# Where the sums of x live and when they are queued: mirrored-exponentials buffers for blocks 3 to 6, a later place for batch 0, and weight sums in sixteen short additions

## The chip, the cores and the metric

The kernel runs on one core of one Trainium2 chip. The metric is device microseconds (us) of one execution; lower is better. A core has a matrix engine (TensorE, PE in the profile, with its weight loads as PEld), a vector engine (VectorE, DVE), an activation engine (ScalarE, ACT), a general engine (GpSimd, POOL) and a queue engine that issues DMAs (SyncE, SP). Each engine works through its own list of instructions in order: an instruction that waits holds up everything queued behind it on that engine.

## The reference, cut to what matters

```python
# attention, per batch of 8: z [3008, 64], u and v [3008, 256]
scores = (1.0 / S) * np.matmul(z, z.transpose(0, 2, 1))
attn = np.maximum(scores, 0.0) ** 2
x = u * np.matmul(attn, v)                         # [8, 3008, 256]
# mixer on x: over tokens, then over channels
h = np.maximum(x.transpose(0, 2, 1) @ w_tok1, 0.0) @ w_tok2     # w_tok1 [3008, 256]
u2 = x + h.transpose(0, 2, 1)
out = u2 + np.maximum(u2 @ w_ch1, 0.0) @ w_ch2                  # w_ch1 [256, 1536]
```

## The kernel before, in words

The work of a batch is cut into six blocks of 512 tokens (the last has 448); block numbers q run from 0 to 5 in the code, so "blocks 3 to 6" of the title are q = 2 to 5. For each block the scores against six groups of keys are made on PE (`sc`, L439), passed through ReLU on ACT into tiles `at` (L477, L465) and squared on DVE in place (L485, L517). The score matrix is symmetric, so from batch 1 on (in batch 0 all are computed) a tile above the diagonal is also transposed by a DMA into a tile `fl` (L537, function `flip`) and used a second time for the mirrored block; these are the "mirrored exponentials" of the change's short title. PE multiplies the tiles with v (`acc`, L668). DVE adds the two halves of the result (`cp`, L805) and multiplies by the transposed u (`xT`, L825). A DMA transpose on SP turns each block of xT into x (L854, function `turn_x`).

The mixer of a batch then runs in pieces on PE. The token product `tok1` (L965) multiplies x by w_tok1, seven products of 128x128 tiles in the place of eight, for each pair of token tiles; it is six pieces, one for each block, of 14 matmuls each. The seven products need sums of the four sub-blocks of x and of the weights. The sums of x are four short subtractions on DVE for each block, each needing the one before (L885, function `x_sums`), into a tile `d`. The sums of the weights are made once (L917 to L920, function `token_sums`) from w_tok1 into `w_sum_sb`. When the six pieces of tok1 are done, `collect_a` (L977) gathers the result on DVE into `a_sb` (seven instructions, L988 to L994); then come the six pieces of `tok2` (L1012), then ReLU layers `hp` (L1066) and the channel products, `xb` and `zb` (L1194) by sums of their own (`hsum`, L1145 to L1157) and `op` (L1280); the results are added up in tiles `ro` (L1231).

From batch 1 on, x is turned only when the v buffers of the batch come free, at the end of its last block, and all six blocks are turned one behind the other. In that stage PE works off the rest of the mixer of the batch before (its blocks 3 to 5: hp, xb, zb), then tok1, collect_a and tok2 of its own batch with what is left of that rest in between.

The order on all engines is fixed when the program is built, by a planner in the kernel. PE's clock is kept in `pe[0]`; work for ACT, DVE and SP is put into lists by `push(engine, ready, busy, lat, fn, first, room, done, frees)`, and `next_op` takes the operation that can start first (the largest `first` wins a tie, so operations with `first=-1` fill what is left). `room` names buffer pools that must have a free place, or a test. An operation of the mixer is a `Piece` with the events that it `needs`; PE takes the next piece whose events are due, and goes on in the same list (`heads` for tok1 and tok2, `tails` for the rest) while one is `opened`: tok1 opens with its first piece and closes with its last. A planned time is a guess: `turn_x` counts 7.5 us from issue to landing (12.0 for the last block). The instruction itself waits for the real event.

The pools that matter here, as `ROOM` has them: `xd`, two buffers for sums of x; `h2`, five; `fl`, ten, for mirrored tiles, for hsum, for ro, for the scratch of collect_a and, in batch 0, for v. In batch 0 the sums of q = 0 to 3 lie two by two in `h2` tiles (`d_pair`); all others take an `xd` buffer each, so that from batch 1 on the sums of q = 2 need tok1 of q = 0 to be over, and so on:

```python
        push("dve", t, 0.21, 0.36, lambda t: x_sums(b, q, t), first=-1,
             room=() if in_h2(b, q) else ("xd",))
...
            live["xd"] -= not in_h2(b, q)          # at the end of tok1 of block q
```

Of the kernel before, what the change touches and what calls it, by code (L numbers as in the profile page):

```python
# [9 lines left out]
BF16 = mybir.dt.bfloat16  # L10
# [3 lines left out]
P = 128  # L14
# [43 lines left out]
def kernel(  # L58
# [11 lines left out]
    nc = tc.nc  # L70
# [4 lines left out]
    KT = (S + P - 1) // P  # L75
# [5 lines left out]
    NQ = (S + QW - 1) // QW  # L81
# [6 lines left out]
    sb = ctx.enter_context(tc.tile_pool(name="sb", bufs=2))  # L88
    psum = ctx.enter_context(tc.tile_pool(name="psum", bufs=2, space=bass.MemoryType.PSUM))
    first = ctx.enter_context(ExitStack())  # L90
# [12 lines left out]
    w_sum_sb = consts.tile([P, 3, KT // 2, P], BF16)  # L103
# [221 lines left out]
    live = {"at": 0, "fl": 0, "xT": 0, "xd": 0, "h2": 0, "us": 0}  # L325
    ROOM = {"at": 6, "fl": 10, "xT": 9, "xd": 2, "h2": 5, "us": 2}
    v_free = [NG]
    at_free = [0.0] * ROOM["at"]
    fl_free = [0.0] * ROOM["fl"]
    ring = [(Done(0.0), i) for i in range(RING)]  # L330
# [7 lines left out]
    def push(engine, ready, busy, lat, fn, first=0, room=(), done=None, frees=()):  # L338
        op = Op(ready, busy, lat, fn, first, room, done, frees)
        waiting[engine].append(op)  # L340
        return op.done
# [34 lines left out]
    pe = [0.0]  # L376
# [165 lines left out]
    def release(name, uses, t=0.0):  # L542
        uses[0] -= 1
        uses[1:] = [max([t] + uses[1:])]
        if not uses[0]:
            live[name] -= 1
            if name == "at":
                at_free.append(uses[1])
            if name == "fl":
                fl_free.append(uses[1])  # L550
# [283 lines left out]
            push("sp", t, 1.25, 7.5 if q < NQ - 1 else 12.0, lambda t: turn_x(b, q, t), first=1,  # L834
                 room=lambda: b == 0 or (mode[0] == "full" and v_free[0] > 0))

    x_pair, d_pair = [], []

    def in_h2(b, q):

        return b == 0 and q < NQ - 2

    def turn_x(b, q, t):

        if b == 0:
            if q % 2 == 0:
                x_pair[:] = [sb.tile([P, 2, DT, QW // P, P], BF16, tag="h2", name="x_pair",
                                     bufs=ROOM["h2"])]
                live["h2"] += 1
            x = x_pair[0][:, q % 2]  # L850
        else:
            x = sb.tile([P, DT, QW // P, P], BF16, tag="v", name="x_sb", bufs=NG)
            v_free[0] -= 1
        nc.sync.dma_start_transpose(  # L854
            out=x.rearrange("p h t d -> p (h t) d"),
            in_=xTs[b, q].rearrange("p h s -> p (h s)"))
        xs[b, q] = x
        x_done[b, q].t = t
        push("dve", t, 0.21, 0.36, lambda t: x_sums(b, q, t), first=-1,
             room=() if in_h2(b, q) else ("xd",))  # L860

    xds = {}
    xd_done = {(b, q): Done() for b in range(B) for q in range(NQ)}

    def x_sums(b, q, t):


        shape = [P, 3, QW // P // 2, P]
        if in_h2(b, q):
            if q % 2 == 0:  # L870
                d_pair[:] = [sb.tile([P, 2] + shape[1:], BF16, tag="h2", name="d_pair",
                                     bufs=ROOM["h2"])]
                live["h2"] += 1
            d = d_pair[0][:, q % 2]
        else:
            live["xd"] += 1
            d = sb.tile(shape, BF16, tag="xd", name="xd", bufs=ROOM["xd"])
        xds[b, q] = d
        v = xs[b, q].rearrange("p n (j r) d -> p n j r d", r=2)
        low, high = v[:, :, :, 0, :], v[:, :, :, 1, :]  # L880
        steps = [(d[:, 1], high[:, 1], low[:, 1]), (low[:, 1], low[:, 1], low[:, 0]),
                 (d[:, 0], high[:, 1], low[:, 1]), (d[:, 2], high[:, 0], d[:, 0])]

        def step(t):
            nc.vector.tensor_sub(*steps.pop(0))  # L885
            if steps:
                push("dve", t - 0.1, 0.21, 0.36, step, first=-1,
                     done=None if len(steps) > 1 else xd_done[b, q])

        step(t)  # L890
# [18 lines left out]
    mix_done, tok_mix_done = Done(), Done()  # L909
    eaten = {b: 0 for b in range(B)}  # L910

    def token_sums(t):


        w = w_tok1_sb.rearrange("p (j r) (m t) -> p j r m t", r=2, t=P)
        low, high = w[:, :, 0], w[:, :, 1]
        nc.vector.tensor_sub(w_sum_sb[:, 0], low[:, :, 0, :], low[:, :, 1, :])  # L917
        nc.vector.tensor_sub(w_sum_sb[:, 1], high[:, :, 1, :], w_sum_sb[:, 0])
        nc.vector.tensor_sub(w_sum_sb[:, 2], high[:, :, 0, :], w_sum_sb[:, 1])
        nc.vector.tensor_add(low[:, :, 1, :], low[:, :, 1, :], high[:, :, 1, :])  # L920
    late_sums = []

    def mix_weights(t):
# [9 lines left out]
    def add_mixer(b):  # L933
# [8 lines left out]
        def tok1(q, end):  # L942

            if q == 0:
                st["a_slot"], _ = take_slot()
                st["a_ps"] = bank_pair(st["a_slot"], "a_ps").rearrange(
                    "p r (k d) -> p r k d", d=P)
            a_ps = st["a_ps"]
            x, d = xs.pop((b, q)), xds.pop((b, q))
            w = w_tok1_sb.rearrange("p (j r) (m t) -> p j r m t", r=2, t=P)  # L950
            n = QW // P // 2
            xp = x.rearrange("p n (j r) d -> p n j r d", r=2)
            for i in range(n):
                j = q * n + i
                products = [
                    ((0, 0), w[:, j, 0, 0, :], xp[:, 0, i, 0, :]),
                    ((0, 1), w[:, j, 1, 0, :], xp[:, 0, i, 1, :]),
                    ((1, 1), w[:, j, 0, 1, :], xp[:, 1, i, 0, :]),
                    ((0, 2), w_sum_sb[:, 1, j, :], d[:, 0, i, :]),
                    ((1, 2), w_sum_sb[:, 0, j, :], d[:, 1, i, :]),  # L960
                    ((0, 3), w_sum_sb[:, 2, j, :], xp[:, 1, i, 1, :]),
                    ((1, 0), w[:, j, 1, 1, :], d[:, 2, i, :]),
                ]
                for (r, k), lhs, rhs in products:
                    nc.tensor.matmul(  # L965
                        a_ps[:, r, k, :], lhs, rhs, start=(j == 0 and (r, k) in ((0, 0), (1, 1))),
                        stop=(j == KT // 2 - 1), skip_group_check=True)
            live["xd"] -= not in_h2(b, q)
            if b == 0:
                live["h2"] -= q % 2 * (1 + in_h2(b, q))  # L970
            else:
                v_free[0] += 1
            eaten[b] = q + 1
            if q == NQ - 1:
                home = "fl" if b else "h2"

                def collect_a(t):  # L977
                    live[home] += 1
                    if b:
                        fl_free.pop(0)  # L980
                    f = sb.tile([P, 8, P], F32, tag=home, name="a_f", bufs=ROOM[home])

                    def both(to, ps, k):
                        nc.vector.tensor_add(  # L984
                            f[:, to:to + 2, :], ps,
                            f[:, k:k + 1, :].to_broadcast([P, 2, P]))

                    nc.vector.tensor_copy(f[:, 6, :], a_ps[:, 0, 0, :])  # L988
                    both(0, a_ps[:, 0, 1:3, :], 6)
                    both(4, a_ps[:, 1, 1:3, :], 1)  # L990
                    nc.vector.tensor_add(f[:, 1, :], a_ps[:, 0, 3, :], f[:, 4, :])
                    both(2, a_ps[:, 1, 0:2, :], 5)
                    st["a"] = sb.tile([P, 2, D], BF16, tag="a", name="a_sb", bufs=1)
                    nc.vector.tensor_single_scalar(  # L994
                        st["a"].rearrange("p m d -> p (m d)"),
                        f[:, 0:4, :].rearrange("p k d -> p (k d)"), 0.0, AX.max)
                    recent[0] = st["a"][:, 0, :1]
                    a_done.t = t
                    if b:
                        release("fl", [1], t)  # L1000
                    else:
                        live["h2"] -= 1
                ring.append((push("dve", end + 0.21, 1.7, 1.9, collect_a, first=1,
                                  room=(home,), frees=fl_free if b else ()), st["a_slot"]))

        def tok2(q, end):
# [318 lines left out]
        for q in range(NQ):  # L1325
            heads.append(Piece(0.784, [x_done[b, NQ - 1], xd_done[b, q], tok_mix_done],
                               lambda end, q=q: tok1(q, end),
                               opens=q < NQ - 1, closes=q > 0, key=(b, 0)))
        for q in range(NQ):
            heads.append(Piece(4 * column_time(widths[q]), [a_done, tok2_done[q]],  # L1330
                               lambda end, q=q: tok2(q, end), key=(b, 1)))
# [269 lines left out]
    def ask_w_tok1(c):  # L1601
        load_w_tok1(c)
        if c == NG - 1:
            push("dve", pe[0] + 16.0, 3.9, 4.1, token_sums, done=tok_mix_done)

    def ask_w_tok2(c):
        load_w_tok2(c)
# [42 lines left out]
    while cur[0] is not None or heads or tails:  # L1650
        run_engines(pe[0])
        ask_some()
        t = pe[0]
# [15 lines left out]
        n = can_score(done_units, most)  # L1669
# [12 lines left out]
        low = lead <= 3  # L1682
# [42 lines left out]
        if pick is None:  # L1725
# [4 lines left out]
            op = next_op()  # L1730
# [15 lines left out]
        elif pick == "av":  # L1746
            step = (blk.b * NQ + blk.q) * NG + blk.slot
# [40 lines left out]
```

## Time and profile before

| | before |
|---|---|
| Median of 3 runs | 1145.62 us (1144.76 to 1146.49) |
| The profiled execution | 1146.74 us |
| Its span, first to last instruction | 1144.9 us |
| PE busy | 1124.2 us (98%) |
| DVE busy | 792.3 us (69%), 1832 instructions |
| ACT busy | 656.7 us (57%) |
| POOL busy | 153.0 us (13%) |
| Mean granted TensorE clock | 0.998 |

How to read it: the span is the profiled execution's own, and 1.84 us of its time lie outside of it. A busy PE is not a PE that issues at its full rate, since a matmul counts as busy until its modelled end; the starts of matmuls, one to the next, tell more. In lists of groups, a line has the engine, the operation, out<-in, the count, then busy time and the mean of one in ns, then the idle time of the engine before them and what ended it. In a timeline, a line has the start, the length, the engine, the line of the kernel and, in brackets, the idle time of that engine just before and what ended it.

### The profile page before, as it was taken

How to read it: one execution, taken by the hardware profiler on the slowest of the kernel's cores; microseconds unless marked ns; L12 is line 12 of the kernel's file. 1: busy time of each engine (PE TensorE's matmuls, PEld its weight loads, DVE VectorE, ACT ScalarE, POOL GpSimd, SP SyncE). 2: the span in 40 equal slices, each digit the busy share in tenths (PEclk: the TensorE clock that was granted, in tenths of full speed). 3: DMA queues.
4: the chain of work that ended last, by engine and by line, in shares of the span. 5: the costliest groups of instructions: out<-in, count | busy, mean ns of one | idle time of the engine just before them, and what ended most of it. 6: DMA issues, size and time to landing. Idle time of an engine off the chain costs nothing.

```text
span 1144.9 us, 26936 instructions
## 1 busy us (share of the span) xinstructions
PE 1124.2 (98%) x10965; PEld 679.7 (59%) x10965; DVE 792.3 (69%) x1832; ACT 656.7 (57%) x818; POOL 153.0 (13%) x387
## 2 busy tenths in 40 slices
PE   9899999999999999999999999999999999999998
PEld 3445565666557665576655765557655576556676
DVE  6788855785757857588566785567756777556874
ACT  7879635535855358544675456653577526744354
POOL 4500010122001220022100221002210111000000
PEclk9999999999999999999999999999999999999999
DMA  9997954996749968699696988969787697474123
GB/s 162 179 169 134 199 114 97 175 181 133 168 100 185 175 128 167 112 201 168 113 158 133 194 156 132 163 118 195 138 163 152 118 195 149 116 150 94 52 70 80
DMA packets 464620, 165.52 MB, mean 145 GB/s; under 512 B 433072, under 2 KB 446960, under 8 KB 464496
## 3 DMA queue, kind: packets, MB, share of 16 engines
q1 hardware_dynamic: 436640, 131.11, 57.3%
q0 software_dynamic: 27344, 32.32, 20.7%
q8 instruction: 85, 1.39, 0.5%
q10 hardware_dynamic: 512, 0.38, 0.1%
q14 instruction: 39, 0.32, 0.1%
HBM read 65.40 MB, written 24.64 MB: 79 GB/s over the span
## 4 chain that ended last, share of the span: by engine, by line
PE 88%; DVE 5%; DMA 5%; ACT 1%; issue 1%; SPq 0%; POOL 0%; DVEq 0%; ACTq 0%
PE acc L668 37%; PE hp L1066 21%; PE xb L1194 10%; PE zb L1194 7%; PE sc L439 6%; PE h_ps L1012 3%; DMA x_pair<-xT 2%; PE a_ps L965 2%; PE op L1280 2%; DVE xd L885 1%; DMA fl<-at 1%; PE first_acc L584 1%; DVE a_f L984 1%; ACT at L477 1%; DMA zT<-zr 1%
## 5 line engine op out<-in xcount | busy, mean ns | idle before, releaser
L1104 ACT ACTIVATE h2pre<-hp 128x1024 bf16<-128x1024 f32 (+1 forms) x278 | 268.8, 1009 | 281.6 <-PE hp L1066 252.8
L668 PEld LDWEIGHTS <-v_sb 64*128 64x128 bf16 x4418 | 241.7, 94 | 221.5 <-issue 7.4
L477 ACT ACTIVATE at<-sc 128x1024 bf16<-128x1024 f32 (+1 forms) x290 | 288.7, 1027 | 95.4 <-PE sc L439 80.4
L668 PE MATMUL acc<-at,v_sb 64*128 64x512 bf16 (+1 forms) x2738 | 339.3, 375 | 3.9 <-DVE at L485 3.8
L485 DVE TENSOR_TENSOR at<-at 128x1024 bf16<-128x1024 bf16 (+1 forms) x290 | 197.0, 687 | 124.1 <-ACT at L477 120.3
L1066 PE MATMUL hp<-xT,w_ch_sb 128*128 128x512 bf16 (+1 forms) x1152 | 271.5, 375 | 0.0
L668 PE MATMUL acc<-fl,v_sb 64*128 64x512 bf16 (+1 forms) x1680 | 190.8, 367 | 0.7 <-ACT at L477 0.7
L1066 PEld LDWEIGHTS <-w_ch_sb 128*128 128x128 bf16 x1152 | 105.9, 98 | 98.4 <-issue 3.1
L439 PE MATMUL sc<-zT 64*128 64x512 bf16 (+1 forms) x732 | 132.3, 361 | 3.2 <-DVE cp L805 1.2
L1194 PEld LDWEIGHTS <-hsum 128*128 128x128 bf16 x1944 | 116.3, 98 | 21.2 <-issue 1.1
L1194 PEld LDWEIGHTS <-h2pre 128*128 128x128 bf16 x1458 | 88.7, 98 | 20.9 <-ACT h2pre L1104 0.7
L465 ACT ACTIVATE at<-sc 128x512 bf16<-128x512 f32 (+3 forms) x152 | 56.0, 444 | 48.9 <-PE sc L439 43.3
L799 ACT COPY cp<-acc 128x512 f32<-128x512 f32 (+1 forms) x94 | 54.7, 585 | 49.4 <-PE acc L668 48.4
L805 DVE TENSOR_TENSOR cp<-acc,cp 128x512 f32<-128x512 f32 (+1 forms) x94 | 63.3, 674 | 24.8 <-ACT cp L799 23.9
L1231 DVE TENSOR_TENSOR ro<-xb,u_sb 128x256 f32<-128x256 f32 (+1 forms) x132 | 53.0, 401 | 39.5 <-PE xb L1194 39.1
L1145 DVE TENSOR_TENSOR hsum<-h2pre 128x512 bf16<-128x512 bf16 (+1 forms) x132 | 53.8, 411 | 34.8 <-ACT h2pre L1104 34.1
L517 DVE TENSOR_TENSOR at<-at 128x512 bf16<-128x512 bf16 (+3 forms) x152 | 41.8, 321 | 47.1 <-ACT at L465 47.1
L439 PEld LDWEIGHTS <-zT 64*128 64x128 bf16 x732 | 42.8, 94 | 47.6 <-issue 8.5
L1194 PE MATMUL xb<-w_mix_sb,hsum 128*128 128x128 bf16 x972 | 68.8, 219 | 0.3
L825 DVE TENSOR_TENSOR xT<-cp,uT 128x512 bf16<-128x512 f32 (+1 forms) x94 | 62.3, 663 | 0.9
L1021 DVE TENSOR_TENSOR xT<-xT,h_ps 128x1024 bf16<-128x1024 bf16 (+1 forms) x48 | 55.4, 1169 | 0.9 <-PE h_ps L1012 0.6
L1157 DVE TENSOR_TENSOR hsum<-h2pre,hsum 128x512 bf16<-128x512 bf16 (+1 forms) x132 | 53.0, 401 | 3.2
(100 smaller groups left out, 930.0 us busy)
## 6 DMA issues: line engine op xcount, KB each, us to landing
out_dram<-ro SPq DMA_DIRECT2D x37, 512.0 KB, 2.9
v_sb<-in_v_dram POOLq DMA_DIRECT2D x40, 256.0 KB, 5.2
ur<-in_u_dram POOLq DMA_DIRECT2D x40, 256.0 KB, 5.9
w_tok_sb<-in_moe_w_tok_dram POOLq DMA_DIRECT2D x10, 256.0 KB, 9.7
zs<-in_z_dram POOLq DMA_DIRECT2D x35, 64.0 KB, 3.5
at<-at SPq DMA_TRANSPOSE x114, 2.4
out_dram<-ro SPq DMA_DIRECT2D x7, 256.0 KB, 2.5
fl<-at SPq DMA_TRANSPOSE x105, 4.9
```

The costliest lines, as they stand in the source:

```text
L439: nc.tensor.matmul(sc[:, r, c0:c1], zT[h, k:k + P], zT[h, m + c0:m + c1], start=True, stop=True)
L465: nc.scalar.activation(a3[:, i, c0:c1], sc[:, r, c0:c1], ACT.Relu, scale=inv_S)
L477: nc.scalar.activation(view, sv, ACT.Relu, scale=inv_S)
L485: nc.vector.tensor_mul(view, view, view)
L668: nc.tensor.matmul(o, vs[blk.b, g][rows, i, dh * P:(dh + 1) * P], rhs, start=(dh, h) not in blk.begun, stop=stop, skip_group_check=True)
L799: nc.scalar.copy(cp[:, :W], acc[:, 1, :W])
L805: nc.vector.tensor_add(cp[:, :W], acc[:, 0, :W], cp[:, :W])
L825: nc.vector.tensor_mul(xT[:, dh, :full * P].rearrange("p (t s) -> p t s", s=P), acc[:, :full * P].rearrange("p (t s) -> p t s", s=P), uT[: ...
L1021: nc.vector.tensor_add(to, to, h[:, :, :n * P].rearrange("p h (s t) -> p h t s", t=n))
L1066: nc.tensor.matmul(hp[:, r, :W], w_ch1_sb[:, dc, cc * P:(cc + 1) * P], xT[:, dc, :W], start=(dc == 0), stop=(dc == DT - 1))
L1104: nc.scalar.activation(h2[:, :, :W], hp[:, :, :W], ACT.Relu)
L1194: nc.tensor.matmul(to[:, i * P:(i + 1) * P], lhs, weights[:, c2, :], start=(first_use and c2 == 0 and i == 0), stop=(c2 == CHT // 2 - 1), ...
```

## The change

Four things change.

1. From batch 1 on, the sums of x of q = 2 to 5 take their buffers two by two from the `fl` pool (`d_pairs`), when at most six of its ten are in use; q = 0 and 1 keep `xd`. A pair is given back when tok1 of its odd block is over. Batch 0 keeps its places.
2. The planner gets the sums of x later than the planned landing of their transpose: by 10 us for q = 0 to 3 of batch 0, by 3 us for q = 4 of batch 0 and for q = 0 to 4 of the other batches, by nothing for q = 5.
3. The weight sums, four instructions of 1536 elements, become sixteen of 384, queued one behind the other with `first=-1`, and 24 us in the place of 16 us after the last of w_tok1 is asked for.
4. The planner counts 2.2 us (2.4 to its end) for collect_a in the place of 1.7 (1.9).

```diff
-    x_pair, d_pair = [], []
-
-    def in_h2(b, q):
-
-        return b == 0 and q < NQ - 2
+    x_pair, d_pairs = [], {}
+
+    def xd_home(b, q):
+
+        if b == 0:
+            return "h2" if q < NQ - 2 else "xd"
+        return "fl" if q >= 2 else "xd"
...
-        push("dve", t, 0.21, 0.36, lambda t: x_sums(b, q, t), first=-1,
-             room=() if in_h2(b, q) else ("xd",))
+        slack = 0.0 if q == NQ - 1 else 3.0 if b or q == NQ - 2 else 10.0
+        push("dve", t + slack, 0.21, 0.36, lambda t: x_sums(b, q, t), first=-1,
+             room=sums_room(b, q))
...
+    def sums_room(b, q):
+
+        if b == 0 and q < NQ - 2:
+            return ()
+        if b == 0 or q < 2:
+            return ("xd",)
+        if q % 2 == 0:
+            return lambda: live["fl"] < ROOM["fl"] - 3
+        return lambda: (b, q - 1) in xds
+
     def x_sums(b, q, t):
...
         shape = [P, 3, QW // P // 2, P]
-        if in_h2(b, q):
-            if q % 2 == 0:
-                d_pair[:] = [sb.tile([P, 2] + shape[1:], BF16, tag="h2", name="d_pair",
-                                     bufs=ROOM["h2"])]
-                live["h2"] += 1
-            d = d_pair[0][:, q % 2]
-        else:
+        home = xd_home(b, q)
+        if home == "xd":
             live["xd"] += 1
             d = sb.tile(shape, BF16, tag="xd", name="xd", bufs=ROOM["xd"])
+        else:
+            if q % 2 == 0:
+                d_pairs[b, q] = sb.tile([P, 2] + shape[1:], BF16, tag=home, name="d_pair",
+                                        bufs=ROOM[home])
+                live[home] += 1
+                if home == "fl":
+                    fl_free.pop(0)
+            d = d_pairs[b, q - q % 2][:, q % 2]
...
-        low, high = w[:, :, 0], w[:, :, 1]
-        nc.vector.tensor_sub(w_sum_sb[:, 0], low[:, :, 0, :], low[:, :, 1, :])
-        nc.vector.tensor_sub(w_sum_sb[:, 1], high[:, :, 1, :], w_sum_sb[:, 0])
-        nc.vector.tensor_sub(w_sum_sb[:, 2], high[:, :, 0, :], w_sum_sb[:, 1])
-        nc.vector.tensor_add(low[:, :, 1, :], low[:, :, 1, :], high[:, :, 1, :])
+        n = KT // 8
+        steps = []
+        for c in range(4):
+            low, high = w[:, c * n:c * n + n, 0], w[:, c * n:c * n + n, 1]
+            to = w_sum_sb[:, :, c * n:c * n + n, :]
+            steps += [
+                (nc.vector.tensor_sub, to[:, 0], low[:, :, 0, :], low[:, :, 1, :]),
+                (nc.vector.tensor_sub, to[:, 1], high[:, :, 1, :], to[:, 0]),
+                (nc.vector.tensor_sub, to[:, 2], high[:, :, 0, :], to[:, 1]),
+                (nc.vector.tensor_add, low[:, :, 1, :], low[:, :, 1, :], high[:, :, 1, :])]
+
+        def step(t):
+            op, *tensors = steps.pop(0)
+            op(*tensors)
+            if steps:
+                push("dve", t, 0.28, 0.42, step, first=-1,
+                     done=None if len(steps) > 1 else tok_mix_done)
+
+        step(t)
...
-            live["xd"] -= not in_h2(b, q)
+            home = xd_home(b, q)
+            if home == "xd":
+                live["xd"] -= 1
+            elif q % 2:
+                release(home, [1], end + 0.2)
             if b == 0:
-                live["h2"] -= q % 2 * (1 + in_h2(b, q))
+                live["h2"] -= q % 2
...
-                ring.append((push("dve", end + 0.21, 1.7, 1.9, collect_a, first=1,
+                ring.append((push("dve", end + 0.21, 2.2, 2.4, collect_a, first=1,
...
-            push("dve", pe[0] + 16.0, 3.9, 4.1, token_sums, done=tok_mix_done)
+            push("dve", pe[0] + 24.0, 0.28, 0.42, token_sums, first=-1)
```

## The prediction

> **What bounds the kernel now.** First the page: how much of the span is PE's, and what the chain of work that ended last runs through.
>
> ```profile
> PE 1124.2 (98%) x10965; PEld 679.7 (59%) x10965; DVE 792.3 (69%) x1832; ACT 656.7 (57%) x818; POOL 153.0 (13%) x387
> ...
> PE 88%; DVE 5%; DMA 5%; ACT 1%; issue 1%; SPq 0%; POOL 0%; DVEq 0%; ACTq 0%
> PE acc L668 37%; PE hp L1066 21%; PE xb L1194 10%; PE zb L1194 7%; PE sc L439 6%; PE h_ps L1012 3%; DMA x_pair<-xT 2%; PE a_ps L965 2%; PE op L1280 2%; DVE xd L885 1%; DMA fl<-at 1%; PE first_acc L584 1%; DVE a_f L984 1%; ACT at L477 1%; DMA zT<-zr 1%
> ```
>
> PE bounds it, so a change can gain only time in which PE doesn't issue. Two names on the chain belong to the change: the transpose of x in batch 0 (`x_pair<-xT`) and the sums (`xd L885`). So next the timeline around the transpose of block 1, which the chain shows issued at 41.78 and 13.78 us under way.
>
> ```profile
> 45.06 1.03 PE L668 MATMUL acc<-at,v_sb 64*128 64x512 bf16 x8
> ...
> 53.26 0.38 PE L439 MATMUL sc<-zT 64*128 64x512 bf16 x2
> ...
> 55.59 0.29 DVE L885 TENSOR_TENSOR d_pair<-x_pair 128x256 bf16<-128x256 bf16 x1 [4.90 <-DMA x_pair<-xT]
> ...
> 57.13 0.61 PE L668 MATMUL acc<-at,v_sb 64*128 64x512 bf16 x4 [3.50 <-DVE at L485]
> ...
> 58.34 0.56 PE L439 MATMUL sc<-zT 64*128 64x512 bf16 x2 [0.59 <-DVE cp L805]
> ...
> 58.65 1.95 PE L668 MATMUL acc<-at,v_sb 64*128 64x512 bf16 x8
> ```
>
> A subtraction stands at the head of DVE's queue for 4.90 us, waiting for a transpose that the planner had expected after 7.5 us. Behind it are a gate (L825) and squares (L485), and PE waits for those. Eight matmuls that took 1.03 us before take 1.95 after, which the busy times by stretch explain (the third figure from the end is the granted clock):
>
> ```profile
> 59.00:60.00 1.00, 1.00 (x8) 0.43 (x6) 1.00 (x3) 0.95 (x1) 0.11 (x2) 0.50 1.23 198
> ```
>
> The granted clock is 0.50 here; from 58.4 to 61.9 us the matmuls run at half pace. The same happens once more, milder, at block 2's transpose (11.64 us under way; DVE stands 1.69 us):
>
> ```profile
> 72.11 0.40 PE L439 MATMUL sc<-zT 64*128 64x512 bf16 x2
> 72.78 0.61 PE L668 MATMUL acc<-at,v_sb 64*128 64x512 bf16 x4 [0.28 <-DVE at L485]
> 73.98 0.39 PE L439 MATMUL sc<-zT 64*128 64x512 bf16 x2 [0.59 <-DVE cp L805]
> ```
>
> Then PE's timeline in a token stage, batch 3's; those of batches 1 to 7 look alike.
>
> ```profile
> 507.50 0.33 PE L965 MATMUL a_ps<-x_sb,w_tok_sb 128*128 128x128 bf16 x3
> ...
> 510.25 0.92 PE L1066 MATMUL hp<-xT,w_ch_sb 128*128 128x448 bf16 x4
> 511.01 0.36 PE L965 MATMUL a_ps<-x_sb,w_tok_sb 128*128 128x128 bf16 x3
> ...
> 514.57 0.92 PE L1066 MATMUL hp<-xT,w_ch_sb 128*128 128x448 bf16 x4
> 515.33 1.57 PE L1280 MATMUL op<-w_ch_sb,h2pre 128*128 128x256 bf16 x12
> 517.16 1.04 PE L1012 MATMUL h_ps<-w_tok_sb,a_sb 128*128 128x512 bf16 x4 [0.26 <-DVE a_sb L994]
> ```
>
> DVE's timeline of the same stretch says why tok1 is not one run:
>
> ```profile
> 508.49 0.29 DVE L885 TENSOR_TENSOR xd<-x_sb 128x256 bf16<-128x256 bf16 x1 [1.78 <-PE a_ps L965]
> ```
>
> The sums of q = 2 wait for a buffer that tok1 of q = 0 holds, though x landed long ago (turned at 481 to 491 us). DVE idles 1.78 us and then makes sixteen subtractions in a row while PE eats them as they come.
>
> **The change part by part.**
>
> *The first stall.* The pair of score matmuls at 53.26 takes one step of 0.22 us (two run at once; 8 matmuls 1.03 us with their tail, 0.86 from start to start). From 53.48 to 57.13: 3.65 us lost. Four matmuls take 0.43, to 57.56; the next starts at 58.34: 0.78. The half clock lasts 3.41 us and costs half of that, 1.71. Sum 6.1 us. The change queues these subtractions 10 us later. DVE came to the first at 50.69, 8.9 us after the issue; at 18.9 us it is past the landing (13.8) by 5 us. So all 6.1 us go.
>
> *The second stall.* 72.33 to 72.78, and 73.21 to 73.98: 0.45 + 0.77 = 1.2 us. DVE came to it 10.0 us after the issue; at 20 us it is past 11.6. The transposes stay where they are in program order; with PE some 6 us earlier, its issue moves from 59.6 to about 54 us, into the stretch where DMA is busiest. Even if it landed no sooner than now (71.2 us), 54 + 20 = 74 is later. What else is late then? The gate of block 3 needs uT, landed at 62.1 us and used at 71.4; of block 5, landed at 81.9 and used at 96.0: margins of 9 and 14 us against 7 us of shift. Nothing near is due sooner.
>
> *Sums in `fl`.* In batch 0, whose sums are ready, the 84 matmuls of tok1 take 4.65 us from first to last start (chain: 120.16, 4.80 us with the tail). Batch 3 takes 507.50 to 514.52, 7.02 us, with one hp piece of 0.76 in it: 7.02 - 4.65 - 0.76 = 1.61 us lost. Batches 1 to 7 start and end 6.96 to 7.02 us apart, each with one hp piece: 7 x 1.61 = 11.3 us. With sums in hand it goes, except for a seam that I set at 0.15 a batch (DVE finishing the last block's sums, which get no slack): 1.0 back. The four subtractions of each block stay four; they move from 508.5-514.1 to about 494-507, behind x's landing plus 3 us. What they land in:
>
> ```profile
> 490.00:495.00 5.00, 5.00 (x61) 3.76 (x59) 4.91 (x18) 3.12 (x4) 2.69 (x6) 1.00 0.71 131
> 495.00:500.00 5.00, 5.00 (x52) 3.38 (x50) 4.09 (x14) 2.95 (x3) 0.00 (x0) 1.00 1.22 203
> 500.00:505.00 5.00, 5.00 (x65) 3.92 (x63) 3.87 (x12) 2.76 (x4) 1.43 (x4) 1.00 1.24 262
> ```
>
> (Third busy figure: DVE.) Sixteen subtractions of 0.285 are 4.6 us; free from 495 to 510 are 15 - 4.09 - 3.87 - 2.56 (505 to 510) = 4.5. It just fits, at the lowest priority, one short instruction at a time. What is queued behind each is an hsum or ro addition, for which xb and zb wait: I charge one subtraction, 0.3 us, a batch, 2.1 in all; the bounds are 0 and the whole 1.6.
>
> *The collect.* After tok1, PE has an hp piece (0.76) and an op piece (12 x 0.109, from 48 in 5.24 us on the chain: 1.31) for the 2.59 us from 514.57 to 517.16: 0.52 us lost, 3.6 over seven batches. With tok1 in one run the hp piece of 510.25 is still there to fill it: 0.76 + 0.76 + 1.31 = 2.83 > 2.59. The longer planned time only makes the planner use it. Gain 3.6.
>
> *The two `fl` buffers* are held from about 494 to tok1's fourth and sixth piece, some 18 us. By the timeline, 505 to 513 us has two to four mirrored tiles, up to three hsum and one ro in `fl`, at most 8 of 10; with two pairs at most 10. Slots are already waited for, by SP, off the path:
>
> ```profile
> SPq L537 <- PE zb L1194: 3.2, 1, 3.2
> ```
>
> A mirrored tile that is issued later is used only at 570 us or after; I take 0 for it, and price the same wait on DVE as a rival.
>
> *Weight sums.* By the rows, a DVE addition takes 0.285 us at 256 elements, 0.42 at 512, 0.955 at 1536, so 0.35 at 384: 16 x 0.35 = 5.6 against 4 x 0.955 = 3.8, 1.8 us more of DVE. They are due before 120 us, and the four long ones at 77 to 81 us stopped no PE. But from 80 to 100 us DVE is busy 19.49 of 20 us. The bounds are 0 and 1.8; I take half, 0.9, as DVE is full there but the sums go last.
> [...]
>
> *Sum.* 6.1 + 1.2 + 11.3 + 3.6 = 22.2 us lost by PE now; back 1.0 + 2.1 + 0.9 = 4.0. Gain 18.2: a span of 1126.7. The median lies 0.7 us above the profiled span (that execution, with 1.84 us around the span, was 1.1 above the median): 1127.4.
>
> **The rivals.**
>
> *Only the early stalls go.* If `fl` has seven or more in use until tok1 begins, the sums are made as late as now: 1145.6 - 7.3 = 1138.3. For it: hsum of two blocks overlap, 6 tiles. Against: by 496 us only four or five buffers hold anything.
>
> *The early stall moves.* With 6 us less slack another DVE instruction may meet a late transfer while DMA is full (until 76 us); uT took 18.1 us once. Price: up to the 4 us of such a stand with the clock; with the 4.0 already charged, 1131.5. Against: the margins above.
>
> *Slower: a slot wait on DVE.* The first subtraction of a pair writes the slot freed longest ago; if its last reader is as late as for SP above, DVE stands 3.2 us with hsum and ro behind it, twice a batch: 14 x 3.2 = 44.8, less 22.2: 1168. It decides above 22.2 / 14 = 1.6 us a pair. For it: SP's waits. Against: with six or fewer in use four slots are free, the oldest for some us.
>
> *Nothing comes of it*: shifts elsewhere in the plan (mirrored tiles landing late cost 0.7 us at 600 and 1.5 at 745) eat the gain: 1145.
>
> **How the numbers follow.** About 0.2%, 2.3 us, is what a measurement of this kernel can tell from no change. The forecast has 0.56; only the early stalls 0.15; the moved stall 0.16; slower 0.09; nothing 0.04. The first three are faster: 0.87. The range goes from all 22.2 us gained, with 1 us for the plan's luck, 1122.5, to the early stalls alone, 1139; the forecast's own is 1123 to 1132.
>
> **What would show it.** After: no wait of DVE on `x_pair<-xT` and no stretch at clock 0.5 in the first 100 us; tok1 as 84 matmuls in 4.7 to 4.9 us in each batch; no idle before `h_ps`; DVE at 95% in the 15 us before tok1. It is wrong if L885 waits on PE or a DMA for over 1 us, if hsum's first addition waits for a slot, or if PE idles in the stage ahead of tok1.

## The result, and the profile after

| | before | after |
|---|---|---|
| Median of the runs | 1145.19 us (6 runs, 1144.36 to 1148.09) | 1135.38 us (6 runs, 1125.69 to 1138.64) |
| Ratio after / before | | 0.9896, 95% interval 0.985 to 0.9942 |
| Profiled execution, its span | 1146.74 us, 1144.9 us | 1138.5 us, 1136.7 us |

The kernel is faster by 9.8 us and inside the range of 1122.5 to 1139.0. But the forecast was 1127.4, and its own range, 1123 to 1132, was missed. The executions spread by 4 us before and by 13 us after; in the rounds of the experiments the kernel before spread by 6 to 16 us as well, so the spread alone says little. The ratios here and below leave out executions more than 1.5% above the fastest of their kernel; the medians and ranges take them in. Two questions stand: where did 8 us of the gain go, and why not in every execution?

First the page of the changed kernel: the engines and the chain of waits (which could be followed back to 509.5 us only, 55% of the span).

```profile
PE 1117.3 (98%) x10965; PEld 677.5 (60%) x10965; DVE 788.0 (69%) x1844; ACT 655.7 (58%) x818; POOL 153.7 (14%) x387
...
PE acc L668 21%; PE hp L1100 12%; PE xb L1228 6%; PE zb L1228 5%; PE sc L439 3%; PE h_ps L1046 2%; PE a_ps L995 2%; DMA u_sb<-xT 1%; PE op L1314 1%; DVE xT L1055 1%; ACT h2pre L1138 0%; DVE ro L1265 0%; DVE res L1348 0%; DMA out_dram<-res 0%; DVE hsum L1184 0%
```

`x_pair<-xT` and `xd` are not on the part that could be followed. It doesn't reach the first 100 us; for those, DVE's waits tell: none is on `x_pair` any more (block 2's transpose lands at 72.9 us, and DVE comes to it at 74.3). A name is on the chain that the views of before did not have: `u_sb<-xT`, the transpose of a block of u2 (x with tok2's result added), which `ro` (L1265) needs.

The PE timeline where the first stall was (start, length, instruction, count), and the busy times of 59 to 60 us (granted clock third from the end):

```profile
53.46 1.89 PE L668 MATMUL acc<-at,v_sb 64*128 64x512 bf16 x16
```

```profile
59.00:60.00 1.00, 1.00 (x14) 0.52 (x10) 0.78 (x2) 1.00 (x2) 0.53 (x1) 1.00 1.20 193
```

No stop, and the clock is 1.00 where it was 0.50. Counted as in the prediction, by the starts of matmuls against their shortest step, PE loses nothing from 52 to 76 us (7.3 us before). Then the end of tok1 in batch 3, which began at 500.48:

```profile
505.11 0.22 PE L995 MATMUL a_ps<-d_pair,w_tok_sb 128*128 128x128 bf16 x1
505.17 1.68 PE L1100 MATMUL hp<-xT,w_ch_sb 128*128 128x448 bf16 x8
506.68 1.67 PE L1314 MATMUL op<-w_ch_sb,h2pre 128*128 128x256 bf16 x12
508.18 1.03 PE L1046 MATMUL h_ps<-w_tok_sb,a_sb 128*128 128x512 bf16 x4
```

84 matmuls start within 4.63 us in every batch; two hp pieces and one op piece follow, and h_ps comes without idle time. The loss lies further on, behind tok2. Batch 5, on PE and on DVE, and the clock after it:

```profile
800.75 1.03 PE L1100 MATMUL hp<-xT,w_ch_sb 128*128 128x512 bf16 x4
806.00 0.61 PE L1228 MATMUL xb<-w_mix_sb,hsum 128*128 128x128 bf16 x8 [4.23 <-DVE ro L1265]
```

```profile
805.53 0.42 DVE L1265 TENSOR_TENSOR ro<-xb,u_sb 128x256 f32<-128x256 f32 x1 [5.17 <-DMA u_sb<-xT]
```

```profile
807.00:809.00 2.00, 1.99 (x17) 1.81 (x18) 1.26 (x4) 0.00 (x0) 0.53 (x1) 0.52 0.24 31
```

`ro` stands at the head of DVE's queue for 5.17 us; the hsum additions behind it come late, and xb on PE waits for those. Half clock follows for 3.41 us. PE loses time in the same place in batches 2, 3, 4 and 6 as well, less of it and with the clock left at 1.00. Together PE loses 13.4 us in these five places (2.45, 1.99, 1.29, 6.61, 1.06), against 0.9 us before. In this execution the first 20 us cost 1.9 us more as well: PE waits 2.23 us for the first transpose of z at 9.5 us, and the clock is 0.50 from 11.8 to 15.2 us.

Why is u_sb late? SP's timeline in that stage, first before, then after. SPq lines have the time that SP was held by issuing the instructions, x3 being three in a row:

```profile
790.80 10.98 SPq L537 DMA_TRANSPOSE fl<-at  x3
...
805.26 1.25 SPq L1035 DMA_TRANSPOSE u_sb<-xT  x1
```

```profile
778.60 16.39 SPq L537 DMA_TRANSPOSE fl<-at  x3
...
799.26 2.00 SPq L1069 DMA_TRANSPOSE u_sb<-xT  x1
```

Against tok1's start (787.77 before, 777.40 after), the three mirrored transposes begin at 3.0 and 1.2 us. They hold SP for 10.98 and 16.39 us, and u_sb behind them is issued at 17.5 and 21.9 and lands at 20.7 and 28.0 us. The landing is 7.3 us later: 4.4 by the later issue, 2.9 by a slower transfer. DVE came to the `ro` that needs it 24.8 us behind tok1's start before, a margin of 4.0 us:

```profile
812.53 0.42 DVE L1231 TENSOR_TENSOR ro<-xb,u_sb 128x256 f32<-128x256 f32 x1
```

It comes to it at 23.0 now (805.53 less 5.17, from 777.40), as the stage is 1.8 us shorter. Over batches 1 to 6 the three transposes take 11.1 us in the mean before and 14.4 after. These are not waits for a buffer. Where SP waits, for the result that a store of `ro` needs, a gap of up to 11.7 us stands before the instruction; here each transpose begins 0.1 us behind the instruction ahead of it and is itself long. The middle one of the three holds SP for 8.07 us (its length in ns, shortest, median and longest of one):

```profile
L537 SPq DMA_TRANSPOSE fl<-at x1: 8065/8065/8065, 782.2 to 782.2; - x1
```

One more thing has moved, the first load of the next batch's v on POOL, from 5.2 us behind tok1's start to 1.7 us in batches 2 to 5:

```profile
793.01 0.53 POOL L218 DMA_DIRECT2D v_sb<-in_v_dram  x1
```

```profile
779.06 0.53 POOL L218 DMA_DIRECT2D v_sb<-in_v_dram  x1
```

### The profile page after: what moved, and what is told of

The parts are those of the page before. It is cut to its first block, busy times and chain, and to the rows that moved or that the text cites. A ratio compares the mean times of both kernels' runs of the same rounds, so it can differ in the third digit from the quotient of the medians.

```text
span 1136.7 us, 26923 instructions
## 1 busy us (share of the span) xinstructions
PE 1117.3 (98%) x10965; PEld 677.5 (60%) x10965; DVE 788.0 (69%) x1844; ACT 655.7 (58%) x818; POOL 153.7 (14%) x387
## 4 chain that ended last, share of the span: by engine, by line
PE 51%; DMA 2%; DVE 2%; ACT 0%; issue 0%; SPq 0%; DVEq 0%; ACTq 0%
PE acc L668 21%; PE hp L1100 12%; PE xb L1228 6%; PE zb L1228 5%; PE sc L439 3%; PE h_ps L1046 2%; PE a_ps L995 2%; DMA u_sb<-xT 1%; PE op L1314 1%; DVE xT L1055 1%; ACT h2pre L1138 0%; DVE ro L1265 0%; DVE res L1348 0%; DMA out_dram<-res 0%; DVE hsum L1184 0%
## 5 line engine op out<-in xcount | busy, mean ns | idle before, releaser
L1265 DVE TENSOR_TENSOR ro<-xb,u_sb 128x256 f32<-128x256 f32 (+1 forms) x132 | 53.0, 401 | 49.2 <-PE xb L1228 36.3
L124 POOL CAST mark<-at 128x1 f32<-128x1 bf16 x12 | 2.9, 243 | 387.8 <-DVE at L485 387.8
```

## The experiments

Four explanations were open for the late u_sb. *Queue*: it stands in SP's order behind mirrored transposes that are slow to issue. *Loads*: these are slow because the loads of v come earlier. *Buffers*: they are slow because the sums hold two of `fl`'s buffers. *Pace*: PE is simply earlier.

| kernel | ratio to before, 95% interval |
|---|---|
| changed kernel, again | 0.9885 (0.9838 to 0.9931) |
| early_only | 0.9931 (0.9912 to 0.995) |
| xd2 | 0.9908 (0.9872 to 0.9943) |
| fl_only | 0.9948 (0.9915 to 0.9981) |
| collect_short | 0.9919 (0.9885 to 0.9954) |
| vlate3 | 0.9863 (0.9815 to 0.9912) |
| v_later | 0.9871 (0.9826 to 0.9916) |
| both_later | 0.9844 (0.9798 to 0.989) |
| fliplate | 0.983 (0.9783 to 0.9877) |
| fliplate_again | 0.9827 (0.9808 to 0.9846) |
| fliplate_wsum4 | 0.9832 (0.9761 to 0.9903) |

### The changed kernel again

> The changed kernel again, unchanged. Its six executions so far lie between 1125.7 and 1138.6 us while the kernel before stays within 4 us. All theories that put the lost 8 us on late transposes u_sb (below) say that the spread is that loss: the idle time of PE after tok2 of batches 2 to 6, 12 to 13 us in the profiled execution of 1138.5 us, and near nothing in one of 1126 us. So of this profile: time = 1126 us plus that idle time, within 1.5 us; median of the executions 1130 to 1138.

1135.88 us (1128.83 to 1144.38). The profiled execution took 1137.67 us. The stall is there, in another place: batch 5 has none now, but in batch 4 three mirrored transposes hold SP for 19.54 us, u_sb lands 31.0 us behind tok1's start, PE idles 6.41 us and runs 6.83 us at half clock. Batches 2, 3 and 4 lose 11.3 us; with them taken off, 1126.4 remain. So the loss differs from one execution to the next, and with it the time.

### Early parts alone

early_only is xd2 with the second edit as well:

```diff
-        return "fl" if q >= 2 else "xd"                  # xd2, and the room test to match
+        return "xd"
-   push("dve", end + 0.21, 2.2, 2.4, collect_a, ...     # early_only
+   push("dve", end + 0.21, 1.7, 1.9, collect_a, ...
```

> The early parts alone: sums of batches 1 to 7 go back to the two xd buffers, batch 0's stay queued later and the weight sums in sixteen. By the prediction's terms the two early stalls (6.1 + 1.2 us) and no more go: 1145.2 - 7.3 = 1137.9 us; tok1 lasts 6.96 to 7.02 us again in batches 1 to 7. All theories of the late u_sb expect no wait of ro for u_sb above 0.5 us, since tok1 is as long as before.

> xd2 with the collect's planned time at 1.7 us as before: nothing is left of the change but batch 0's later queueing and the weight sums in sixteen. The prediction's 7.3 us: 1137.9 us against 1145.2, a ratio of 0.9936; no stall at 52 to 76 us. If the collect's planned time is worth what xd2 suggests (7 x 0.43 = 3.0 us), this kernel is some 3 us slower than xd2, and 0.52 us a batch are lost again before h_ps.

early_only took 1137.94 us (1137.67 to 1140.48); the prediction's term gave 1137.9. Nothing is lost from 52 to 76 us, tok1 takes 7.02 us again, and 0.52 us a batch are lost before h_ps. xd2 took 1136.53 us. tok1 is as long, but only 0.09 us is lost before h_ps: the planner puts xb and zb pieces there. So early_only is 1.4 us slower where some 3 were expected, and the two intervals overlap. `ro` waited for u_sb 0.7 us at most.

### The collect

> The changed kernel, but the planner's time for the collect stays at 1.7 us as before (2.2 in the change). The prediction's step: with tok1 in one run there is enough PE work at hand, so h_ps starts without idling anyway: 0.2 us or less lost between tok1 and h_ps in each batch. Rival, from xd2, where tok1 was not in one run and yet only 0.09 us was lost: it is the longer planned time that makes the planner put work there, and without it 0.4 to 0.6 us a batch are lost again. The time: as the changed kernel by the first, 2 to 3 us more by the second, which the spread of the executions hides; the profile decides.

The edit is early_only's second one, in the changed kernel. The loss before h_ps is 0.19 us in six of seven batches, as with 2.2 us planned. Batch 1 alone has the rival's picture (PE timeline), 1.10 us lost:

```profile
232.54 1.68 PE L1100 MATMUL hp<-xT,w_ch_sb 128*128 128x448 bf16 x8
235.16 1.04 PE L1046 MATMUL h_ps<-w_tok_sb,a_sb 128*128 128x512 bf16 x4 [0.94 <-DVE a_sb L1028]
```

So the prediction's step holds for six batches: with tok1 in one run there is enough work at hand. In the seventh it takes the longer planned time for the planner to add the op piece. The time, 1139.2 us, is that of the changed kernel within the spread; this profile has an early stall of its own, 5.9 us.

### Sums in fl alone

```diff
-        slack = 0.0 if q == NQ - 1 else 3.0 if b or q == NQ - 2 else 10.0
+        slack = 0.0 if q == NQ - 1 or b == 0 else 3.0
         # and token_sums in four long instructions, due as before
```

> Sums in fl alone: blocks 3 to 6 of batches 1 to 7 keep the new buffers and the collect its longer planned time, while batch 0's sums are queued at once as before and the weight sums are four long instructions again. By the prediction's terms the two early stalls (7.3 us) come back and 11.3 + 3.6 - 1.0 - 2.1 = 11.8 us stay, less the 8 or so that the late u_sb take: between 1145.2 - 11.8 = 1133.4 (no late u_sb) and 1142 us. The profile: a DVE wait on the transpose x_pair at 45 to 60 us with PE idle and a granted clock of 0.5 behind it, tok1 in one run, ro waiting for u_sb after some batches.

1143.39 us is above the 1142 expected, but the kernel before stood at 1147.28 in this round; by the ratio it is 6.0 us faster (2.2 to 9.7), within what was expected for some late u_sb. The early stall is back on DVE's timeline, to a hundredth of before's 4.90:

```profile
54.69 0.29 DVE L901 TENSOR_TENSOR d_pair<-x_pair 128x256 bf16<-128x256 bf16 x1 [4.89 <-DMA x_pair<-xT]
```

52 to 76 us lose 6.8 us. Behind tok2 of batch 2 PE idles 5.39 us for `ro` and runs 3.41 us at half clock, 7.1 us lost. So the late u_sb belongs to the sums in `fl` and the shorter stage, not to batch 0's part.

### The loads of v

```diff
-        ask(lambda: load_v(b + 1, c), lambda: eaten[b] > j)
+        ask(lambda: load_v(b + 1, c), lambda: eaten[b] > j and pe[0] > ate_at[b, j] + 2.5)  # vlate3
+        ask(lambda: load_v(b + 1, c), lambda: eaten[b] > j and pe[0] > ate_at[b, 0] + 8.0)  # v_later
```

> The changed kernel, but each load of the next batch's v waits until 2.5 us after tok1 has eaten its buffer, which puts it where it was before against tok1's start. Loads theory (these 1 MB or so of loads, 2 to 3.6 us earlier than before, slow the transposes on SP): u_sb of q = 0 lands 2 us or more sooner, PE's idle time after tok2 falls from 12 to under 4 us, median 1126 to 1130. Queue theory without the loads, buffer theory and pace theory: idle time and median as in the changed kernel, 1133 to 1138.

The threshold hardly took effect: the first load stays at 1.7 us in batches 2 to 5, and only some later loads of batches 1 and 6 and a few instructions behind them changed place. So this tells nothing of the loads; it is nearly the changed kernel once more, 1132.33 us, with 1.6 us lost at u_sb in the profiled execution of 1128.3 us.

> The changed kernel, but the planner holds the next batch's loads of v until 8 us after tok1 has eaten the first block, so that each is asked for some 4.5 us later (in vlate3 the threshold of 2.5 us had no effect: the loads were issued at the same times as in the changed kernel, so that run is the changed kernel once more). Loads theory: the first mirrored transpose of the stage is issued in 2.5 to 4 us instead of 5, u_sb of q = 0 lands 2 us or more sooner in most batches, PE's idle time after tok2 is under 1 us in all batches together, median 1125 to 1129. Queue theory without the loads: mirrored transposes as slow as in the changed kernel, u_sb at 24 to 28 us from tok1's start in several batches, 1130 to 1138.

Here the first load does move, to 8.0 to 8.3 us. SP in batch 5 and that load on POOL (tok1 begins at 774.62):

```profile
777.25 11.45 SPq L537 DMA_TRANSPOSE fl<-at  x3
...
792.21 1.25 SPq L1071 DMA_TRANSPOSE u_sb<-xT  x1
```

```profile
782.87 0.54 POOL L218 DMA_DIRECT2D v_sb<-in_v_dram  x1
```

The three transposes take 9.1 us in the mean of six batches (7.4 to 11.5), against 14.4, 13.3 and 12.3 in the changed kernel's two profiles and vlate3's; the sums lie in the same `fl` buffers, and PE's order from tok1 to tok2 is the same (it differs in the blocks behind the stage, and some transposes of u on SP moved). PE idles 1.8 us in all behind tok2 (forecast by loads: under 1), in batches 3 and 4, where u_sb still lands at 24.5 and 25.0 us. The median, 1132.43 us, is not below vlate3's: the execution time alone does not show the gain within this spread, the transposes do. Nor is it a later start that helps: in batches 1 and 2 the transposes begin 1.1 us behind tok1's start and take 7.6 us each time, where the changed kernel's, begun at 1.1 and 1.8 us, took 11.7 and 14.3. This speaks for loads as one cause, and against buffers. They are not the only cause. In batch 6 the first load comes at 1.2 us in the kernel before as in the changed one, and the next three start at 7.9 us where they started at 5.2 before; yet the transposes take 16.1 us in the profile of the changed kernel, and took 11.7 before.

### Nine buffers

```diff
-    ROOM = {"at": 6, "fl": 10, ...
+    ROOM = {"at": 6, "fl": 9, ...                        # in xd2
```

> xd2 with nine fl buffers instead of ten for the whole program: the shortage of buffers that the sums bring, without the shorter tok1. Buffer theory: SP stands at a mirrored transpose in the token stages (a gap of over 2 us between SP's instructions), and u_sb of q = 0 is issued 2 us or more later than in xd2 (17.6 to 19.5 us from tok1's start there). Queue theory: no such gap, u_sb issued at 17 to 20 us, no ro that waits over 1 us. The time is some 5 us longer by the plan, elsewhere: 1140.

1147.23 us in one execution. SP has no gap in the token stages, its instructions follow each other by some 0.1 us; but in batch 3 the three mirrored transposes hold it for 14.06 us (9.60 in xd2), u_sb is issued 23.9 us behind tok1's start, and PE idles 2.84 us for `ro`. So a shortage of buffers also ends with slow transposes, or the order that the planner makes with nine does; one profile does not tell these apart.

### The mirrored transposes behind u_sb

```diff
     room=lambda: has_room(("fl",)) and (
-        b < 2 or q or x_done[divmod(b * NQ + q - 1, NQ)].t is not None)
+        b < 2 or q or (x_done[divmod(b * NQ + q - 1, NQ)].t is not None
+                       and (u_turned[b - 1] > 1 or eaten[b - 1] == 0)))
     # turn_u2 counts: u_turned[b] += 1
```

PE's planned order is untouched, and the first loads of v stay at 1.7 us.

> The changed kernel, but the mirrored tiles of the next batch's first block are queued on SP only once two u_sb transposes of this batch are. Queue theory (u_sb stands behind mirrored transposes that are slow to be issued): u_sb of q = 0 is issued 3 to 6 us sooner, no ro waits for it over 0.5 us, no idle of PE after tok2, median 1123 to 1128 us with a spread like that of the kernel before. Buffer theory (the mirrored transposes wait for fl buffers that the sums hold): the same here. Pace theory (u_sb takes as long as ever after its issue, and PE is simply 2 us earlier): PE still idles some 12 us, median about 1135. If the mirrored tiles themselves come too late instead, acc waits for fl some 10 us behind the stage, and nothing is gained: 1135 or more.

> fliplate once more, to see whether it beats the changed kernel, whose executions (18 with those of vlate3) lie from 1125.7 to 1144.4 with a median near 1134: queue theory 1124 to 1129 us, no ro that waits over 0.5 us for u_sb; stalls of its own early in the kernel (5.7 us at 89 us in the first look) are chance and don't come back at the same place.

1128.85 us (1125.66 to 1143.08), then 1125.77 us (1124.70 to 1127.57). From the second profile, the engines' line and SP and PE around batch 5's u_sb (tok1 begins at 771.64):

```profile
PE 1112.1 (99%) x10965; PEld 675.3 (60%) x10965; DVE 786.7 (70%) x1844; ACT 655.1 (58%) x818; POOL 153.2 (14%) x387
```

```profile
783.72 1.45 SPq L1071 DMA_TRANSPOSE u_sb<-xT  x1
...
789.90 11.45 SPq L538 DMA_TRANSPOSE fl<-at  x3
```

```profile
794.91 1.03 PE L1103 MATMUL hp<-xT,w_ch_sb 128*128 128x512 bf16 x4
795.78 0.83 PE L1231 MATMUL xb<-w_mix_sb,hsum 128*128 128x128 bf16 x12
```

u_sb is issued 12.1 us behind tok1's start and lands at 17.7 (21.9 and 28.0 in the changed kernel), no `ro` waits for it in any batch, and xb follows hp without idle time. Pace alone is refuted: with the same tok1 the wait is gone. The span is 1122.9 us, 22.0 less than before's. In this second round it is the fastest of the kernels tried, at a ratio of 0.9827 (0.9808 to 0.9846); those of the changed kernel are 0.9896 (0.985 to 0.9942) and 0.9885 (0.9838 to 0.9931), so the intervals meet at their ends. The median of its ten executions is 1127.2 us, that of the changed kernel's twelve 1135.9. The moved transposes are no faster for having been moved: begun 18 to 20 us behind tok1's start, they hold SP for 11.3 to 13.8 us, but u_sb is no longer behind them. The first profile lost 10.6 us between 75 and 100 us: two z transposes held SP for 11.0 us, PE idled 5.68 us, and 6.83 us at half clock followed. It did not come back in the second profile; but collect_short lost 5.9 us in the same way, so 2 of the 12 profiles with the later queueing have a stall there.

> fliplate and v_later together: the mirrored tiles of the next batch's first block behind two u_sb, and the loads of v 4.5 us later. Queue theory: no more to win over fliplate, since nothing waited for u_sb there: 1124 to 1129 us. If the mirrored tiles that were moved collide with the loads that were moved, acc of the next batch waits for fl or v at its beginning, 1130 or more.

1130.61 us (1126.23 to 1149.05), a little above the 1124 to 1129 expected: nothing won over fliplate, as the queue explanation said. The profile shows where the order bites next. In batch 4 a store of `ro` (`out_dram<-ro`) is issued behind the mirrored transposes, its `fl` slot comes free late, an hsum on DVE waits 3.28 us for that slot, and PE idles 2.35 us.

### The weight sums

> fliplate with the weight sums in four long instructions again, the last part of the change that has not been tried by itself; fliplate's executions are close together (1124.7 to 1127.6), so 2 us can be seen here. The prediction's term: sixteen short ones cost 0.9 us of PE (0 to 1.8), so this kernel is 0.9 us faster. Rival: four long ones hold DVE for 3.8 us at a stretch, and an addition or a square behind them comes late, so that it is 1 to 3 us slower, by a stall of PE between 75 and 110 us. Third: neither shows, within 1 us of 1126.

1127.01 us, within 1.3 us of fliplate_again, so the times show neither. The profile shows the loss where the rival put it, DVE and then PE:

```profile
80.44 0.95 DVE L938 TENSOR_TENSOR w_tok_sb<-w_tok_sb 128x1536 bf16<-128x1536 bf16 x1
...
81.92 2.22 DVE L485 TENSOR_TENSOR at<-at 128x896 bf16<-128x896 bf16 x4
```

```profile
82.64 0.39 PE L439 MATMUL sc<-zT 64*128 64x512 bf16 x2 [0.42 <-ACT at L477]
```

The long sums hold DVE from 77.5 to 81.4 us, four squares behind them run in one block, and PE loses 1.5 us from 75 to 100 us against 0.2 in fliplate_again. That is one execution each.

## Why the prediction was right, and where it was wrong

*The early stalls.* Right, 7.3 us. The parts alone gave 1137.94 us where the term gave 1137.9; all of DVE's waits on `x_pair` are gone. The sign "no stretch at clock 0.5 in the first 100 us" failed by its letter, through the wait for z at 9.5 us, which comes ahead of the first sums of x. "The early stall moves" had 0.16. Two profiles of twelve have a stall at 82 to 95 us, where PE itself waits for z, at a price (5.9 and 10.6 us) above the 4 us that were set; the kernel before and fl_only show none there.

*tok1.* Right: 1.61 us a batch went to 0.00. The seam, charged at 1.0, did not show. DVE was busy 95% in the 15 us before tok1, as forecast (14.26 of 15 us from 485.5 to 500.5 in batch 3), and the 2.1 us charged for it did not show either.

*The collect.* Right in kind, 2.3 in place of 3.6 us: by the starts of matmuls 0.52 us a batch became 0.19, where the sum had it go to nothing.

*The weight sums.* Wrong in sign on the one pair of profiles: the four long ones, moved to the later place, cost some 1.3 us, and sixteen short ones none. PE did not wait for the sixteen, longer in sum (16 x 0.350 = 5.6 us against 3.8); it met the length of the block. The additions took 0.350 us for 384 elements and 0.955 for 1536; a straight line through the two leaves an estimated 0.15 us for each instruction, whatever its length.

*The step that failed* is in the part on the two `fl` buffers: "A mirrored tile that is issued later is used only at 570 us or after; I take 0 for it". The use of the tile was looked up, but not what is queued behind it on SP: u_sb, with a margin of 4.0 us in batch 5 (landed 20.7, due 24.8). The mirrored tiles were not issued later either, but earlier, at 1.2 us in place of 3.0, and took longer. The shorter stage takes 1.8 us of the margin, and u_sb's landing, 7.3 us later, takes the rest and makes the wait of 5.17 us. No term of the sum had the u_sb, nor the loads of v that a faster tok1 releases earlier. The loss in the profiled execution is 12.5 us (13.4 less 0.9). The row of SP that the prediction read as a wait for a slot (3.2 us) was a sign of it: that transpose begins at 518.14 us, 0.1 us behind the instruction ahead of it, and holds SP for 3.50 us, so it is a long issue and no wait. The listed sign, PE idle "ahead of tok1", looked at the wrong side of tok1 as well.

*The rivals.* "Slower: a slot wait on DVE" did not happen: no hsum waited for a slot in the changed kernel's list of waits. "Only the early stalls go" has almost the right time, 1138.3, for a wrong reason: tok1 did gain 11.3 us, and u_sb took them back. So it is luck that the time lies inside the range: its upper end was set for a kernel in which tok1 gains nothing.

*The size.* With u_sb out of the way, the 22.2 us of stalls come out as 22.0 us of span, and the time is 1125.8 us, where the forecast, with 4.0 us charged back, said 1127.4. The match of 22.2 and 22.0 is partly luck: the parts as measured are 7.3 + 11.3 + 2.3 = 20.9 us, and the other 1.1 us come from places that the sum did not have.

What stays open: how much of the slower transposes is due to the loads (with later loads they take 9.1 us in the mean, less than the 11.1 before), what else slows them in batch 6, and why one execution meets the stall in batch 5 and the next in batch 4.

## What to carry to other kernels

When a stage gets shorter, list every transfer that is due at its end, with its margin (due time less landing, from the trace), and take the shortening off each margin; what is left below zero is the new stall. Buffers that are eaten sooner also release the next loads sooner, here into the time of those transfers (the first at 1.7 us behind tok1's start in place of 5.2). And where a queue works in order, as SP did here (u_sb of batch 5 was issued behind 16.39 us of mirrored transposes), a transfer with a near due time should not stand behind long ones that are used only some 60 us later: moving three instructions a batch on SP brought the median here from 1135.9 to 1127.2 us.

## What the runs showed of the hardware

The three mirrored transposes of a batch held SP between 7.4 and 19.5 us over all kernels, and those of batch 4 alone 12.2 and 19.5 us in two executions of the changed kernel: issue time was no constant of the instruction here. Later loads of v went with shorter holds (9.1 us in the mean in v_later, 12.3 to 14.4 in three profiles with the earlier loads); what sets them otherwise was not found.

After PE had idled for more than 3 us, the granted clock was 0.50 for 3.41 or 6.83 us each time (idle for 3.48 and 5.39 us in fl_only, 3.50 in the kernel before, 4.23 in the changed kernel, 4.44 in collect_short, 5.68 in fliplate and 6.41 in the changed kernel's second profile). Between 2.2 and 2.9 us it fell in five cases (2.23 in the changed kernel, 2.29 in early_only, 2.35 in both_later, 2.65 in fl_only, 2.84 in xd2_fl9) and not in two (2.68 and 2.81, in collect_short). Single stops of up to 1.9 us left it alone; once it fell after three short ones (0.47, 1.25 and 0.89 us) at the start of fliplate. A stall of 2.35 us so cost about 4 us (both_later, batch 4: 4.2 us more lost than in the same place of fliplate_again). The shortest single stop that lowered the clock here is 2.23 us, the longest that did not 2.81.
